# A three-stage attention, mixture and Mish kernel on one core: the element-wise order of its last layer is rearranged

## Chip, cores and metric

One NeuronCore of a Trainium2 chip runs the whole program. The metric is the device time of one execution in microseconds (us); the median of three executions stands for a kernel. The engines are TensorE (PE), VectorE (DVE), ScalarE (ACT), GpSimd (POOL) and SyncE (SP). Each works through its own instructions in program order and waits on semaphores for the others.

## The reference

Three layers follow each other, all in fp32. Attention (2 batches, 8 heads, 768 positions, head size 64) sees 8 global and 96 local keys. A top-2 mixture of 8 experts (512 to 1024 to 512) takes the 1536 tokens, and the last layer is a dense one of 512 to 2048 to 512 with a Mish activation between its two products:

```python
def _moe2_ref(x, w_in, w_out):
    h = x @ w_in
    sp = np.where(h > 20.0, h, np.log1p(np.exp(np.minimum(h, 20.0))))
    g = h * np.tanh(sp)
    return (g @ w_out).astype(np.float32)
```

The change lies in the last layer alone.

## The kernel before

Every fp32 product is made of three products in the fp32r type: each operand is split into a high part (`hi`, a copy rounded to fp32r on ACT) and a low part (`lo`, the rest, by a subtraction on DVE), and PE adds `hi*hi + hi*lo + lo*hi` (`three`, L856 to L860).

The order of the instructions is written by hand: an engine runs its instructions in the order in which the Python code issues them.

**The last layer** works on 4 blocks of 384 tokens (`tb`), with 16 slices of 128 hidden units (`f`) in each: 64 steps, n = 16 tb + f. `last_in` (L1165) makes the 128x384 pre-activations `hp` of a step with 12 matmuls (L858 to L860). `last_out` (L1217) adds the step's slice into three accumulators with 9 matmuls, six from `hhi` (L1225, L1226) and then three from `hlo` (L1230). The loop (L1246) issues on PE `last_in(n)` and then `last_out(n-2)`, so PE has two steps' work between a step's pre-activations and their use. I write in(n) and out(n) for the two.

**The activation** of a step is a chain over ACT and DVE: exp of `hp` on ACT (`mish_0`, L1181); the minimum with e^20 on DVE (L1185), then on ACT the square (L1186), the logarithm (L1187) and `rexp`, an exponential with a negative sign, which gives a first reciprocal (`mish_2`, L1191); three DVE operations, two of them a Newton step (`mish_3`, L1196 to L1198), the third of which multiplies with `hp` and gives the result; its high part on ACT (`mish_5`, L1201) and its low part on DVE (`mish_6`, L1204). In step n the loop issues, leaving conversions aside:

- on ACT: exp(n), high part of n-1, square(n), logarithm(n), rexp(n);
- on DVE: minimum(n), low part of n-1, the three Newton operations of n.

The first and the last step are cut into thirds of 128 columns (`for_cuts`).

**The weight conversions.** The weights of the last layer come as 64-bit words and are turned into `hi` and `lo` by `w64_begin` (L304): for each half tile of 128x512, four DVE operations (L327 to L330) and then `rest` (L321): a copy on ACT (L322) and two DVE operations (L323, L324). 26 of the 32 halves are made in the layers before; six are left and are made in steps 2 to 13: the first two operations in an even step, the next two and `rest` in the odd step behind it. `w64_load` (L296) fetches the next raw half through SP at the end of each odd step.

**The row sums.** For a block after the first, each token's two expert rows are gathered by POOL (`rows_of`, L866, at f = 2, 6, 10 of the block before), weighted and added (`combine_2`, L1155: ACT L1156, DVE L1157, at f = 5, 9, 13), transposed on PE (`combine_3`, L1159: four PE transposes, L1162, at f = 6, 10, 14) and split into `hi` and `lo` (`split_ps`, L862: ACT L863, DVE L864).

Of the kernel before, what the change touches and what calls it, by code (L numbers as in the profile page):

```python
# [9 lines left out]
F32 = mybir.dt.float32  # L10
# [4 lines left out]
AF = mybir.ActivationFunctionType  # L15
OP = mybir.AluOpType
# [5 lines left out]
P = 128  # L22
# [6 lines left out]
TB = 384  # L29
# [147 lines left out]
def build(tc, ctx, I, out, n_global, n_local, dbg=None):  # L177
    nc = tc.nc
    dbg = dbg or {}
    V, A, G, T = nc.vector, nc.scalar, nc.gpsimd, nc.tensor  # L180
# [115 lines left out]
    def w64_load():  # L296
        j, s = divmod(state["load64"], 2)
        if j < 16:
            state["load64"] += 1
            raws[j, s] = wraw.tile([P, 512, 2], I32, name="raw")  # L300
            nc.sync.dma_start(raws[j, s], I["w_moe2"][j, :, s * 512:(s + 1) * 512].bitcast(I32)
                              .rearrange("p (a b) -> p a b", b=2))

    def w64_begin():  # L304


        j, s = divmod(state["conv"], 2)
        if j == 16:
            return None
        state["conv"] += 1  # L310
        if s == 0:
            pool, n = (wlast, "l") if j < 16 - RING else (wring, "")
            pieces[64 + j] = (pool.tile([P, 1024], F32R, name="whi" + n), pool.tile([P, 1024], F32R, name="wlo" + n))
        raw = raws.pop((j, s))
        lw, uw = raw[:, :, 0], raw[:, :, 1]
        hi, lo = (w[:, s * 512:(s + 1) * 512] for w in pieces[64 + j])
        t1 = wtmp.tile([P, 512], I32, name="t1", bufs=2)
        t2 = wtmp.tile([P, 512], I32, name="t2", bufs=1)
        f1 = t1.bitcast(F32)

        def rest():  # L321
            A.activation(hi, f1, AF.Copy)  # L322
            V.tensor_tensor(f1, f1, hi.bitcast(F32), op=OP.subtract)  # L323
            V.tensor_tensor(lo, f1, lo.bitcast(F32), op=OP.add)  # L324

        return (
            lambda: V.tensor_scalar(t1, uw, 0x07FFFFFF, 3, op0=OP.bitwise_and, op1=OP.logical_shift_left),  # L327
            lambda: V.scalar_tensor_tensor(t1, uw, -0x40000000, t1, op0=OP.bitwise_and, op1=OP.bitwise_or),
            lambda: V.tensor_scalar(t2, t1, -0x800000, None, op0=OP.bitwise_and),
            lambda: V.scalar_tensor_tensor(lo, lw.bitcast(U32), 2.0 ** -52, t2.bitcast(F32), op0=OP.mult, op1=OP.mult),  # L330
            rest,
        )

    xgs, xgT = {}, {}
# [46 lines left out]
    with ExitStack() as st:  # L381
# [440 lines left out]
        for t in range(NT):  # L822
            load_raw(t + 2)
            load_values(t + 1)
            for hp in range(0, HP, PER):
# [5 lines left out]
                k = t * HP // PER + hp // PER  # L831
# [34 lines left out]
    def rows_of(t, k):  # L866
        yg = xg_p.tile([P, DM], F32, name="xg") if k == 0 else mk.tile([P, DM], F32, name="ys", bufs=3)
        G.indirect_dma_start(out=yg, out_offset=None, in_=yd[:(E - 1) * CAP, :] if k == 0 else yd,
                             in_offset=bass.IndirectOffsetOnAxis(ap=cidx[:, k, t:t + 1], axis=0))
        return yg  # L870
# [11 lines left out]
    mk = ctx.enter_context(tc.tile_pool(name="mk", bufs=2))  # L882
# [213 lines left out]
    steps = [(e, f) for e in range(E) for f in range(8)]  # L1096
    lists = []
    half = None
    for n, (e, f) in enumerate(steps):
# [39 lines left out]
        half = w64_begin() if conv else None  # L1139
# [13 lines left out]
    gT, acc2 = {}, {}  # L1153

    def combine_2(t, rows):  # L1155
        A.activation(rows[0], rows[0], AF.Copy, scale=wlh[:, 0, t:t + 1])  # L1156
        V.scalar_tensor_tensor(rows[1], rows[1], wlh[:, 1, t:t + 1], rows[0], op0=OP.mult, op1=OP.add)  # L1157

    def combine_3(t, rows, pool, name):  # L1159
        tp = pool.tile([P, 4, P], F32, name=name)  # L1160
        for d in range(4):
            T.transpose(tp[:, d], rows[1][:, d * P:(d + 1) * P], ident)  # L1162
        combine_4(t, tp)

    def last_in(tb, f):  # L1165
        whi, wlo = (w.rearrange("p (d f) -> p d f", d=4) for w in pieces[64 + f // 2 * 2])
        xhi, xlo = x2T[tb]
        c = (f % 2) * P
        hp = ps_h.tile([P, 512], F32, name="hp")
        for d in range(4):  # L1170
            three(hp[:, :TB], whi[:, d, c:c + P], wlo[:, d, c:c + P], xhi[:, d], xlo[:, d], d == 0, d == 3)
        return hp[:, :TB]
# [1 line left out]


    def mish_begin(hp, n):
        r = mk.tile([P, TB], F32, name="r", bufs=1)
        return hp, vt[:, n % 2, :TB], vt[:, 2 + n % 2, :TB], r

    def mish_0(m, cc):  # L1180
        A.activation(m[1][:, cc], m[0][:, cc], AF.Exp)  # L1181
# [11 lines left out]
    def mish_3(m, cc):  # L1193

        h, v, s, r = (a[:, cc] for a in m)
        V.scalar_tensor_tensor(s, s, 1.0, r, op0=OP.add, op1=OP.mult)  # L1196
        V.scalar_tensor_tensor(s, s, -2.0, r, op0=OP.add, op1=OP.mult)
        V.scalar_tensor_tensor(v, s, 0.5, h, op0=OP.add, op1=OP.mult)  # L1198

    def mish_5(m, g, cc):  # L1200
        A.activation(g[0][:, cc], m[1][:, cc], AF.Copy)  # L1201

    def mish_6(m, g, cc):
        V.tensor_tensor(g[1][:, cc], m[1][:, cc], g[0][:, cc].bitcast(F32), op=OP.subtract)  # L1204

    def mish_end():
        return tuple(mk.tile([P, CAP], F32R, name=n)[:, :TB] for n in ("hhi", "hlo"))
# [4 lines left out]
    def for_cuts(n, stage, *a):  # L1212

        for cc in (THIRDS if n in (0, 16 * NTB - 1) else [ALL]):
            stage(*a, cc)

    def last_out(tb, f):  # L1217
        whi, wlo = (w.rearrange("p (f d) -> p f d", f=2)[:, f % 2] for w in pieces[64 + f // 2 * 2 + 1])
        ghi, glo = gT.pop((tb, f))
        last = (tb, f) == steps[-1]  # L1220
        if f == 0:
            acc2[tb] = [ps_a.tile([P, 512], F32, name="ac") for _ in range(TC)]
        for c in range(TC):
            cc = slice(c * P, (c + 1) * P)
            T.matmul(acc2[tb][c], ghi[:, cc], whi, start=(f == 0), stop=False)  # L1225
            T.matmul(acc2[tb][c], ghi[:, cc], wlo, start=False, stop=False)  # L1226
            if last:
                T.matmul(acc2[tb][c], glo[:, cc], whi, start=False, stop=True)
        for c in (() if last else range(TC)):
            T.matmul(acc2[tb][c], glo[:, c * P:(c + 1) * P], whi, start=False, stop=(f == 15))  # L1230

    def last_store(tb, f):
        if f == 15:
            for c in range(TC):
                os = mk.tile([P, DM], F32, name="ys", bufs=3)
                if c % 2:
                    V.tensor_scalar(os, acc2[tb][c], 2.0, None, op0=OP.mult)
                else:
                    A.activation(os, acc2[tb][c], AF.Copy, scale=2.0)
                r0 = tb * TB + c * P  # L1240
                nc.sync.dma_start(out[r0:r0 + P, :], os)

    steps = [(tb, f) for tb in range(NTB) for f in range(16)]
    m = {}
    vt = mk.tile([P, 4, CAP], F32, name="yT", bufs=1)
    for n in range(len(steps) + 2):  # L1246
        new, old = n < len(steps), 1 <= n <= len(steps)
        if new:
            tb, f = steps[n]
            m[n] = mish_begin(last_in(tb, f), n)  # L1250
        if n >= 2:
            last_out(*steps[n - 2])
        if n % 2 == 0:
            half = w64_begin() if n else None
        if new:
            for_cuts(n, mish_0, m[n])
        if old:
            g = gT[steps[n - 1]] = mish_end()
        if old:
            for_cuts(n - 1, mish_5, m[n - 1], g)  # L1260
        if new:
            for_cuts(n, mish_1, m[n])
        if half:
            half[n % 2 * 2]()
        if new:
            for_cuts(n, mish_2, m[n])
        if old:
            for_cuts(n - 1, mish_6, m[n - 1], g)
        if half:
            half[n % 2 * 2 + 1]()  # L1270
        if new:
            for_cuts(n, mish_3, m[n])
        if late and n:
            late.pop(0)()
        if half and n % 2:
            half[4]()
        if n >= 2:
            last_store(*steps[n - 2])
        if new and tb + 1 < NTB:
            for c in range(TC):  # L1280
                t = TC * (tb + 1) + c
                if f == 2 + 4 * c:
                    rows[t] = [rows_of(t, 0), rows_of(t, 1)]
                if f == 5 + 4 * c:
                    combine_2(t, rows[t])
                if f == 6 + 4 * c:
                    combine_3(t, rows[t], ps_q, "tq")
        if n % 2:
            w64_load()

# [2 lines left out]
    with tc.If(most > CAP):  # L1295
        with tc.tile_pool(name="one", bufs=1) as one:
            for tb in range(NTB):
# [4 lines left out]
                for c in range(TC):  # L1302
# [4 lines left out]
                    for d in range(4):  # L1307
# [4 lines left out]
                                    op0=OP.is_equal, op1=OP.mult)  # L1312
                    V.tensor_scalar(g2, iot[:, :E], chosen[:, 1, t:t + 1], w12[:, 1, t:t + 1],
                                    op0=OP.is_equal, op1=OP.mult)
                    V.tensor_tensor(gate[:, c], gate[:, c], g2, op=OP.add)
                V.memset(ysum, 0.0)
                for e in range(E):
                    ac = [ps_a.tile([P, 512], F32, name="ac") for _ in range(TC)]
                    for g in range(4):
# [4 lines left out]
                        for f in range(2):  # L1324
                            hp = ps_h.tile([P, 512], F32, name="hp")
# [11 lines left out]
                vt = mk.tile([P, 4, CAP], F32, name="yT", bufs=1)  # L1337
# [62 lines left out]
```

## Time and profile before

| | us |
|---|---|
| median of 3 runs | 736.98 (736.25 to 737.54) |
| the profiled execution's own time | 739.06 |
| its span, first to last instruction | 737.2 |
| PE busy in the span | 708.8 (96%) |
| DVE busy | 523.9 (71%) |
| ACT busy | 424.0 (58%) |
| the last layer, first matmul (442.3) to the end of the span | 294.9 |

The times in the rows count from the first instruction of the span. A timeline row gives the start, the duration, the engine, the line, the operation, its output and input, the count, and in brackets the idle time of the engine ahead of it and what ended that. The end of a matmul is modelled, so starts are compared rather than ends. For ACT and DVE the start of the next operation can lie before the end of the one ahead.

### The profile page before, as it was taken

The page shows a single profiled execution, that of the slowest core. Times are in us where ns is not written, and L with a number is a line of the kernel's source. Part 1 is how long each engine was busy: PE and PEld are TensorE (multiplying, and loading weights), DVE is VectorE, ACT ScalarE, POOL GpSimd, SP SyncE. Part 2 cuts the span into 40 slices and gives each one's busy share as a digit, 9 for nine tenths or more (in the row PEclk, how much of TensorE's full clock was granted, in tenths as well). Part 3 has the DMA queues.
Part 4 walks back from the last instruction along what each step waited for, and adds up shares of the span by engine and source line. Part 5 has one row for each costly group of instructions (what it writes and reads, how often), then busy time and mean ns, then how long its engine had stood idle before and what let it go on. Part 6 is the DMA issues. An engine that isn't in the chain of part 4 may idle for free.

```text
span 737.2 us, 11732 instructions
## 1 busy us (share of the span) xinstructions
PE 708.8 (96%) x4259; PEld 643.7 (87%) x4259; DVE 523.9 (71%) x1237; ACT 424.0 (58%) x892; POOL 61.6 (8%) x83
## 2 busy tenths in 40 slices
PE   8999899999999999999999989898999999999995
PEld 4777779999999999999999978787999989989993
DVE  7789769977586676758575876888666666666663
ACT  5899632444444544444444437566667667667663
POOL 2000200301010100101000212100120020000000
PEclk9999899999999999999999999999999999999998
DMA  7799321757475655647454734300120030001001
GB/s 166 217 220 240 127 67 39 244 159 232 161 221 167 198 186 177 221 158 219 151 170 142 236 106 135 112 29 0 56 74 1 0 106 10 0 1 44 1 0 47
DMA packets 42932, 89.26 MB, mean 121 GB/s; under 512 B 5987, under 2 KB 18403, under 8 KB 42868
## 3 DMA queue, kind: packets, MB, share of 16 engines
q1 hardware_dynamic: 35412, 69.37, 31.4%
q0 software_dynamic: 4096, 13.11, 5.9%
q10 hardware_dynamic: 3360, 5.97, 2.1%
q8 instruction: 35, 0.57, 0.3%
q14 instruction: 29, 0.24, 0.1%
HBM read 75.32 MB, written 13.11 MB: 120 GB/s over the span
## 4 chain that ended last, share of the span: by engine, by line
PE 79%; DVE 10%; ACT 6%; DMA 2%; issue 1%; POOL 1%; ACTq 0%; DVEq 0%
PE hp L858 11%; PE hp L859 11%; PE hp L860 11%; PE ac L858 6%; PE ac L860 6%; PE ac L859 6%; PE ac L1225 5%; PE ac L1226 5%; PE ac L1230 4%; PE xp L567 3%; PE tp L554 2%; PE sp L516 2%; PE tq L892 2%; PE tq L934 2%; ACT r L1187 1%
## 5 line engine op out<-in xcount | busy, mean ns | idle before, releaser
L858 PE MATMUL hp<-xgh,whi 128*128 128x416 f32 (+1 forms) x288 | 104.2, 362 | 0.0
L280 DVE TENSOR_TENSOR wlo<-raw,whi 128x1024 fp32r<-128x1024 f32 x61 | 74.6, 1223 | 38.1 <-ACT whi L277 35.9
L859 PE MATMUL hp<-xgl,whi 128*128 128x416 f32 (+1 forms) x288 | 100.6, 349 | 0.2 <-DVE xgl L711 0.2
L860 PE MATMUL hp<-xgh,wlo 128*128 128x416 f32 (+1 forms) x288 | 100.7, 350 | 0.0
L858 PE MATMUL ac<-hhi,whi 128*128 128x416 f32 x256 | 92.0, 359 | 0.0
L859 PE MATMUL ac<-hlo,whi 128*128 128x416 f32 x256 | 90.1, 352 | 0.3 <-DVE hlo L905 0.3
L860 PE MATMUL ac<-hhi,wlo 128*128 128x416 f32 x256 | 90.1, 352 | 0.0
L1196 DVE SCALAR_TENSOR_TENSOR yT<-yT,r 128x384 f32<-128x384 f32 (+1 forms) x68 | 36.4, 535 | 73.9 <-ACT r L1191 69.9
L858 PE MATMUL hp<-xgh,whil 128*128 128x384 f32 x224 | 77.0, 344 | 0.0
L859 PE MATMUL hp<-xgl,whil 128*128 128x384 f32 x224 | 76.4, 341 | 0.0
L904 ACT ACTIVATE hhi<-hp 128x416 fp32r<-128x416 f32 x64 | 33.3, 520 | 74.7 <-PE hp L860 64.6
L860 PE MATMUL hp<-xgh,wlol 128*128 128x384 f32 x224 | 75.9, 339 | 0.0
L277 ACT ACTIVATE whi<-raw 128x1024 fp32r<-128x1024 f32 x61 | 64.4, 1055 | 17.2 <-PE ac L859 12.0
L1225 PE MATMUL ac<-whil,hhi 128*128 128x512 f32 x144 | 57.3, 398 | 1.5 <-ACT hhi L1201 1.3
L1226 PE MATMUL ac<-wlol,hhi 128*128 128x512 f32 x144 | 56.6, 393 | 0.0
L859 PEld LDWEIGHTS hp<-xgl,whi 128*128 128x128 f32 x288 | 54.3, 189 | 1.1 <-DVE xgl L711 0.4
L858 PEld LDWEIGHTS hp<-xgh,whi 128*128 128x128 f32 x288 | 54.2, 188 | 1.1 <-ACT xgh L710 0.4
L1181 ACT ACTIVATE yT<-hp 128x384 f32<-128x384 f32 (+1 forms) x68 | 31.6, 471 | 40.6 <-PE hp L860 37.4
L860 PEld LDWEIGHTS hp<-xgh,wlo 128*128 128x128 f32 x288 | 54.0, 188 | 0.4
L863 ACT ACTIVATE xgh<-tq 128x512 fp32r<-128x512 f32 (+2 forms) x38 | 20.2, 533 | 57.8 <-PE tq L892 57.8
L1201 ACT ACTIVATE hhi<-yT 128x384 fp32r<-128x384 f32 (+1 forms) x68 | 34.5, 507 | 31.7 <-DVE yT L1198 30.7
L905 DVE SCALAR_TENSOR_TENSOR hlo<-hp,hhi 128x416 fp32r<-128x416 f32 x64 | 37.5, 586 | 16.7 <-ACT hhi L904 16.7
(241 smaller groups left out, 1526.2 us busy)
## 6 DMA issues: line engine op xcount, KB each, us to landing
raw<-in_w_moe SPq DMA_DIRECT2D x96, 512.0 KB
yd<-ys ACTq DMA_DIRECT2D x21, 256.0 KB
ks<-in_k_t SPq DMA_DIRECT2D x24, 136.0 KB
qr<-in_q_t SPq DMA_DIRECT2D x24, 128.0 KB
vt<-in_v_w SPq DMA_DIRECT2D x12, 256.0 KB
xd<-xs SPq DMA_DIRECT2D x12, 256.0 KB
out<-ys SPq DMA_DIRECT2D x12, 256.0 KB
vt<-in_v_w SPq DMA_DIRECT2D x10, 208.0 KB
```

Of the source, the lines that this page charges most:

```text
L277: A.activation(hi, raw, AF.Copy)
L280: e_lo.tensor_tensor(lo, raw, hi.bitcast(F32), op=OP.subtract)
L858: T.matmul(ps, whi, xhi, start=first, stop=False)
L859: T.matmul(ps, whi, xlo, start=False, stop=False)
L860: T.matmul(ps, wlo, xhi, start=False, stop=last)
L904: A.activation(hhi, hp[:, :CAP], AF.Relu)
L905: V.scalar_tensor_tensor(hlo, hp[:, :CAP], 0.0, hhi.bitcast(F32), op0=OP.max, op1=OP.subtract)
L1181: A.activation(m[1][:, cc], m[0][:, cc], AF.Exp)
L1196: V.scalar_tensor_tensor(s, s, 1.0, r, op0=OP.add, op1=OP.mult)
L1201: A.activation(g[0][:, cc], m[1][:, cc], AF.Copy)
L1225: T.matmul(acc2[tb][c], ghi[:, cc], whi, start=(f == 0), stop=False)
L1226: T.matmul(acc2[tb][c], ghi[:, cc], wlo, start=False, stop=False)
```

## The change

Three things of the last layer's loop are rearranged; no operation is added or taken away.

1. The Newton operations and the high part of step n-1 are issued in step n behind the minimum (DVE) and behind rexp (ACT) of step n (`newton`). On ACT a step is now exp(n), square(n), logarithm(n), rexp(n), high part of n-1; on DVE it is minimum(n), Newton of n-1, a conversion operation, low part of n-1, one or two conversion operations. For step 0 Newton stays ahead of the minimum of step 1. The buffers follow: one buffer for exp's output, two for the result, which now stays in the square's buffer, and two for rexp's.
2. The conversions are one list of operations, taken one or two at a time (`convert`): per step one DVE operation ahead of the low part and one behind it, two behind it in every third step, from step 1 on. The ACT copy of a half (`high`) goes with its third operation. The raw half that follows is fetched when a half is begun.
3. `combine_2` is issued at f = 4, 8, 12 instead of 5, 9, 13.

```diff
+        def high():
             A.activation(hi, f1, AF.Copy)
-            V.tensor_tensor(f1, f1, hi.bitcast(F32), op=OP.subtract)
-            V.tensor_tensor(lo, f1, lo.bitcast(F32), op=OP.add)
+        low = (
+            lambda: V.tensor_tensor(f1, f1, hi.bitcast(F32), op=OP.subtract),
+            lambda: V.tensor_tensor(lo, f1, lo.bitcast(F32), op=OP.add),
+        )
...
     def mish_begin(hp, n):
-        r = mk.tile([P, TB], F32, name="r", bufs=1)
-        return hp, vt[:, n % 2, :TB], vt[:, 2 + n % 2, :TB], r
+        r = vt[:, 3, :TB] if n % 2 else mk.tile([P, TB], F32, name="r", bufs=1)
+        return hp, vt[:, 0, :TB], vt[:, 1 + n % 2, :TB], r
...
+    def convert(k):
+        for _ in range(k):
+            if not todo:
+                half = w64_begin()
+                if not half:
+                    return
+                w64_load()
+                todo.extend((*half[:2], *half[5:6], *half[2:4], *half[6:]))
+            while todo:
+                op = todo.popleft()
+                op()
+                if op.__name__ != "high":
+                    break
...
+        def newton(x):
+            g = gT[steps[x]] = mish_end()
+            for_cuts(x, mish_3, m[x])
+            for_cuts(x, mish_5, m[x], g)
         if new:
             for_cuts(n, mish_0, m[n])
-        if old:
-            g = gT[steps[n - 1]] = mish_end()
-        if old:
-            for_cuts(n - 1, mish_5, m[n - 1], g)
+        if n == 1:
+            newton(0)
         if new:
             for_cuts(n, mish_1, m[n])
-        if half:
-            half[n % 2 * 2]()
-        if new:
             for_cuts(n, mish_2, m[n])
         if old:
-            for_cuts(n - 1, mish_6, m[n - 1], g)
-        if half:
-            half[n % 2 * 2 + 1]()
-        if new:
-            for_cuts(n, mish_3, m[n])
+            if n > 1:
+                newton(n - 1)
+            convert(1)
+            for_cuts(n - 1, mish_6, m[n - 1], gT[steps[n - 1]])
+            convert(1 + (n % 3 == 0))
...
-                if f == 5 + 4 * c:
+                if f == 4 + 4 * c:
                     combine_2(t, rows[t])
```

## Rows read from the trace of the kernel before

**Rows 1.** Waits, 440 to 520 us, PE: total, times, longest, in us.

```profile
PE tq L1162 <- DVE ys L1157: 6.8, 3, 3.2
```

**Rows 2.** Timeline of PE: the first matmul or transpose of some steps.

```profile
455.07 0.50 PE L1225 MATMUL ac<-whil,hhi 128*128 128x512 f32 x1 [0.59 <-ACT hhi L1201]
...
457.26 0.33 PE L858 MATMUL hp<-xgh,whil 128*128 128x384 f32 x1
...
473.91 0.66 PE L1162 MATMUL tq<-ident,ys 128*128 128x128 f32 x4 [3.17 <-DVE ys L1157]
474.32 0.55 PE L858 MATMUL hp<-xgh,whil 128*128 128x384 f32 x1
...
480.15 0.33 PE L858 MATMUL hp<-xgh,whil 128*128 128x384 f32 x1
...
513.92 0.63 PE L1162 MATMUL tq<-ident,ys 128*128 128x128 f32 x4 [2.31 <-DVE ys L1157]
...
518.58 0.34 PE L858 MATMUL hp<-xgh,whil 128*128 128x384 f32 x1
...
718.22 0.33 PE L858 MATMUL hp<-xgh,whi 128*128 128x384 f32 x1
```

**Rows 3.** Windows: length, busy time (count) of five engines, granted clock, DMA share, GB/s.

```profile
474.00:478.00 4.00, 4.00 (x16) 4.00 (x17) 3.44 (x8) 2.24 (x4) 0.00 (x0) 0.57 0.00 0
...
726.90:730.40 3.50, 3.27 (x7) 2.06 (x7) 1.14 (x3) 0.89 (x3) 0.00 (x0) 0.52 0.21 77
```

**Rows 4.** Timeline of DVE, the end of step 5 and the minimum of step 6.

```profile
473.11 0.75 DVE L1157 SCALAR_TENSOR_TENSOR ys<-ys,wlh,xg 128x512 f32<-128x512 f32 x1
473.77 0.35 DVE L1185 TENSOR_SCALAR yT<-yT 128x384 f32<-128x384 f32 x1
```

**Rows 5.** Timeline of DVE and ACT, steps 12 and 13 (minimum to low part).

```profile
503.73 0.35 DVE L1185 TENSOR_SCALAR yT<-yT 128x384 f32<-128x384 f32 x1
...
504.00 0.42 DVE L327 TENSOR_SCALAR t<-raw 128x512 int32<-128x512 int32 x1
...
504.12 0.62 ACT L1186 ACTIVATE yT<-yT,one 128x384 f32<-128x384 f32 x1 [1.07 <-DVE yT L1185]
...
504.77 0.62 ACT L1187 ACTIVATE r<-yT,one 128x384 f32<-128x384 f32 x1
...
505.43 0.53 ACT L1191 ACTIVATE r<-r 128x384 f32<-128x384 f32 x1
...
505.86 0.48 ACT L1181 ACTIVATE yT<-hp 128x384 f32<-128x384 f32 x1
...
505.98 0.56 DVE L1196 SCALAR_TENSOR_TENSOR yT<-yT,r 128x384 f32<-128x384 f32 x1 [0.49 <-ACT r L1191]
...
507.17 0.55 DVE L1198 SCALAR_TENSOR_TENSOR yT<-yT,hp 128x384 f32<-128x384 f32 x1
...
507.64 0.35 DVE L1185 TENSOR_SCALAR yT<-yT 128x384 f32<-128x384 f32 x1
...
507.76 0.53 ACT L1201 ACTIVATE hhi<-yT 128x384 fp32r<-128x384 f32 x1 [1.43 <-DVE yT L1198]
...
508.32 0.56 DVE L1204 TENSOR_TENSOR hlo<-yT,hhi 128x384 fp32r<-128x384 f32 x1
```

**Rows 6.** Groups of DVE by line, 440 to 520 us: count, busy us, mean ns.

```profile
L324 DVE TENSOR_TENSOR wlo<-t,wlo 128x512 fp32r<-128x512 f32 x6 | 4.2, 693 | 0.2
...
L327 DVE TENSOR_SCALAR t<-raw 128x512 int32<-128x512 int32 x6 | 2.5, 421 | 0.0
```

**Rows 7.** Timeline of ACT and POOL, steps 2 and 3.

```profile
453.07 0.47 ACT L1181 ACTIVATE yT<-hp 128x384 f32<-128x384 f32 x1
...
455.58 1.44 POOL L868 DMA_INDIRECT ys<-yd,cidx  x1 [28.41 <-ACT yT L1186]
```

**Rows 8.** Timeline of the last step's chain: ACT, DVE.

```profile
720.51 0.62 ACT L1181 ACTIVATE yT<-hp 128x128 f32<-128x128 f32 x3 [1.41 <-PE hp L860]
...
723.96 0.29 DVE L1196 SCALAR_TENSOR_TENSOR yT<-yT,r 128x128 f32<-128x128 f32 x1 [1.83 <-ACT r L1191]
```

More of the change, by code (lines that the diff above doesn't have):

```diff
@@ L321, in rest @@
         def rest():
+            high()
+            for op in low:
+                op()
+        def high():
             A.activation(hi, f1, AF.Copy)
-            V.tensor_tensor(f1, f1, hi.bitcast(F32), op=OP.subtract)
-            V.tensor_tensor(lo, f1, lo.bitcast(F32), op=OP.add)
+        low = (
+            lambda: V.tensor_tensor(f1, f1, hi.bitcast(F32), op=OP.subtract),
+            lambda: V.tensor_tensor(lo, f1, lo.bitcast(F32), op=OP.add),
+        )
         return (
@@ L331, in w64_begin @@
             rest,
+            high,
+            *low,
         )
@@ L1197, in mish_3 @@
         V.scalar_tensor_tensor(s, s, -2.0, r, op0=OP.add, op1=OP.mult)
-        V.scalar_tensor_tensor(v, s, 0.5, h, op0=OP.add, op1=OP.mult)
+        V.scalar_tensor_tensor(s, s, 0.5, h, op0=OP.add, op1=OP.mult)
     def mish_5(m, g, cc):
-        A.activation(g[0][:, cc], m[1][:, cc], AF.Copy)
+        A.activation(g[0][:, cc], m[2][:, cc], AF.Copy)
     def mish_6(m, g, cc):
-        V.tensor_tensor(g[1][:, cc], m[1][:, cc], g[0][:, cc].bitcast(F32), op=OP.subtract)
+        V.tensor_tensor(g[1][:, cc], m[2][:, cc], g[0][:, cc].bitcast(F32), op=OP.subtract)
     def mish_end():
@@ L1244, in build @@
     m = {}
+    todo = deque()
+    def convert(k):
[8 more added lines that the diff above has]
+                op = todo.popleft()
+                op()
+                if op.__name__ != "high":
+                    break
     vt = mk.tile([P, 4, CAP], F32, name="yT", bufs=1)
@@ L1252, in build @@
             last_out(*steps[n - 2])
-        if n % 2 == 0:
-            half = w64_begin() if n else None
+        def newton(x):
+            g = gT[steps[x]] = mish_end()
+            for_cuts(x, mish_3, m[x])
+            for_cuts(x, mish_5, m[x], g)
         if new:
             for_cuts(n, mish_0, m[n])
-        if old:
-            g = gT[steps[n - 1]] = mish_end()
-        if old:
-            for_cuts(n - 1, mish_5, m[n - 1], g)
+        if n == 1:
+            newton(0)
         if new:
             for_cuts(n, mish_1, m[n])
-        if half:
-            half[n % 2 * 2]()
-        if new:
             for_cuts(n, mish_2, m[n])
         if old:
-            for_cuts(n - 1, mish_6, m[n - 1], g)
-        if half:
-            half[n % 2 * 2 + 1]()
-        if new:
-            for_cuts(n, mish_3, m[n])
+            if n > 1:
[3 more added lines that the diff above has]
+            convert(1 + (n % 3 == 0))
         if late and n:
             late.pop(0)()
-        if half and n % 2:
-            half[4]()
         if n >= 2:
@@ L1287, in build @@
                     combine_3(t, rows[t], ps_q, "tq")
-        if n % 2:
-            w64_load()
     most = nc.values_load(over[:1, :1], min_val=0, max_val=2 * NTOK)
```

## The prediction, made before the changed kernel ran

> **What bounds the kernel now.** Read first the starts of PE's steps in the last layer. From in(16) at 518.58 to in(63) at 718.22 lie 47 steps and six groups of transposes, in 199.64 us; a group takes 473.91 to 474.32, 0.41 us [rows 2]. So a step costs (199.64 - 6 x 0.41) / 47 = 4.20 us: PE's own work, which nothing in this change shortens. Of it last_out has 457.26 - 455.07 = 2.2 with a late start, 2.1 without, and last_in the other 2.1 [rows 2]. The steps ahead of that are slower: in(4) to in(16) takes 61.32 [rows 2], where 12 x 4.20 + 3 x 0.41 = 51.6 would do. These 9.7 us are all that can be won in the steady part.
>
> Then read which wait ends last there. Three times PE stands before the row-sum transposes, 6.8 us in total, 3.2 the longest [rows 1]; the first ends at 473.91 after 3.17, the last at 513.92 after 2.31 [rows 2], which leaves 1.3 for the middle one. The sum that they wait for (L1157) is the last DVE operation of step 5, 13 or 9, behind both conversion operations of `rest`; it starts at 473.11 and PE at 473.91 [rows 2, 4]. After the longest of these gaps the granted clock was 0.57 over 474 to 478, that is mostly the lower of its two levels [rows 3], and the step from 474.32 to 480.15 took 5.83, 1.6 more than 4.20 [rows 2]. 6.8 + 1.6 = 8.4 of the 9.7; the rest is PE waiting for a high part, like the 0.59 before out(1) [rows 2].
>
> **The change part by part.**
>
> *Row sums moved up.* The sum goes from the end of step 5 to the end of step 4 (so too 9 to 8, 13 to 12), and the transposes stay in step 6, behind out(4), which needs the low part of step 4, made by DVE in step 5, after the sum. So the transposes never wait for the sum by themselves: the 6.8 and the 1.6 go, unless the wait moves to the parts of step 4. The sum's ACT half now stands ahead of exp(5). Its rows are gathered by POOL; the first second-row gather is issued at 455.58 and takes POOL 1.44 [rows 7]. The new sum starts near 465.4, 8.4 us after that. When data land no row shows: I take no cost; at most the sum would run at its old place, one step (4.2 us) later.
>
> *The chain in the new order.* Slots, from one start to the next: ACT from the minimum on: 503.73, 504.12, 504.77, 505.43, 505.86, so 0.39 + 0.65 + 0.66 + 0.43 = 2.13 until the next ACT operation, now the high part of n-1 [rows 5]. DVE beside it: the minimum's slot 504.00 - 503.73 = 0.27, Newton's three 507.17 - 505.98 = 1.19 to the third, and 507.76 - 507.17 = 0.59 from there to the high part: 2.05 [rows 5]. So the high part starts 2.13 after the minimum; the low part can start 508.32 - 507.76 = 0.56 later, and PE too [rows 5]. In the steady part exp starts 720.51 - 718.22 = 2.29 after in(n) starts [rows 2, 8], the minimum some 0.5 later (exp takes 0.47 [rows 7]), and the high part is ready at 2.29 + 0.5 + 2.13 + 0.56 = 5.5; out(n-1) begins 4.20 + 2.1 = 6.3 after in(n). The new wait has 0.8 to spare. Queued behind it on ACT is exp(n+1), due at 6.5; on DVE the low part, which PE needs six matmuls later. So steps 16 to 62 keep 4.20.
>
> *DVE's load in steps 1 to 16.* A slot is about 0.08 shorter than the duration: 0.27 for 0.35, and 507.64 - 507.17 = 0.47 for 0.55 [rows 5]. Conversion: two operations like L327 (0.42) and four like L324 (0.69) per half [rows 6], 3.09 in slots, 0.52 each; 7 in three steps make 1.20 a step. Minimum, Newton, low part: 0.27 + 1.19 + 0.47 + 0.47 = 2.40. Row sum and its split, 0.75 [rows 4] and about 0.69, three times in 16 steps: 0.25. Waiting for the high part: it allows the low part at 2.69 after the minimum, while Newton and one conversion end at 2.3 to 2.5, so 0.25. Total 4.10 against PE's 4.20 + 0.08: enough, barely.
>
> By the Trainium skill ("VectorE: DVE Perf Modes", section "The DRAIN you can't avoid") a VectorE operation starts only when the pipe of the one before is empty, save where it is not held. The trace goes by the exception: 0.27 after a minimum of 0.35 the next one starts [rows 5]. What the rule would give is rival B.
>
> *Start-up.* Newton(1) now follows minimum(2), which follows exp(2). exp(2) started at 453.07 [rows 7], its ACT queue up to there is unchanged. Minimum(2) 453.6, high part(1) 453.6 + 2.13 = 455.7, PE 456.3: out(1) is 1.2 later than 455.07 [rows 2], and in(4) at 458.5 instead of 457.26. Then I lay ACT, DVE and PE out by these slots, operation by operation in the order of the diff, up to in(16). For example step 5: DVE ends step 4 with the sum at 466.1, minimum(5) starts there, high part(4) at 468.2, ready at 468.8, out(4) due at 468.9. The high part of step n-1 comes ahead of its product by 0.4, 0.5, 0.1, 1.0, 0.3, 0.7, 0.5, 0.2, 0.0, 0.7, 0.0, 0.8, 0.7 us in steps 3 to 15. Four of these are thin; I charge 0.5 us for them together (bounds 0 and, were every step late by what rival B has, 2.5). The copy of a half waits on ACT for its second DVE operation where both fall into one batch (step 9), and holds exp(10) up by some 1 us; it costs nothing because out(9) is still met by 0.2. in(16): 458.5 + 12 x 4.20 + 3 x 0.41 + 0.5 = 510.6, against 518.58: **-8.0 us**.
>
> *Tail.* Before, the last step's Newton starts at 723.96, behind rexp [rows 8]. Now the high part of step 62 comes behind rexp(63) rather than ahead of the square: the ACT chain is some 0.4 earlier, its three rexp thirds are through near 723.9, then come the high part of 62 (0.56 until its low part) and the low part (0.47), and only then Newton(63): 724.9, **+0.9**. The window of the last seven matmuls had a granted clock of 0.52 [rows 3]; PE is through with out(61) at 718.22 + 4.20 = 722.4 and gets the high part of 62 at 723.9 + 0.56 = 724.5, so it now idles for 2 us in one piece and the lower level may fall elsewhere. At full clock throughout the 3.27 us of PE in that window would be 1.6 shorter (-0.7 in all), and with half of out(62) slowed too, 1.0 longer (+1.9). I take +0.9, since the rows show the lower level at this place.
>
> *Sum:* -8.0 + 0.9 = -7.1. The profiled execution took 739.06 with a span of 737.2, so it would take 732.0; the median of the runs shown, 736.98, becomes 729.9.
>
> **The rivals.**
>
> *B, DVE paces the first 16 steps.* If each operation took its full duration, DVE would need 0.35 + 1.19 + 0.56 + 0.56 + 7/3 x 0.60 + 0.27 = 4.33, and some 0.1 of waiting, 4.43 against 4.28: 16 x 0.15 = 2.4, so 732.3. Against it: the starts in [rows 5]. For it: the thin steps above. The page named above would have this. Chance 0.16.
>
> *C, the clock falls in the start-up.* PE idles some 2.0 us before out(1) instead of 0.59 [rows 2]. A gap of 3.17 was followed by the lower level, at a price of 1.6; one of 2.31 was not known to be (513.92 to 518.58 is 4.66, as 4.20 + 0.41) [rows 2, 3]. 731.5. Chance 0.13.
>
> *D, the wait only changes its name.* Transposes no longer wait, but the high parts come late, or the gathered rows do, and by 0.4 us a step over 16 steps the loop gives 6.4 back: 736.3. It is what the step times of before look like where conversions crowd one step in two. Against it: the loads above. Chance 0.07.
>
> *E, slower.* The high part now stands behind rexp(n), so PE's wait hangs on the chain of the step itself: 5.5 of 6.3 us. Should the chain take 6.3 + 0.19 or more, each of the 48 later steps is late by as much, 48 x 0.19 = 9.1, which eats the 7.1 and puts the time at 739.0; from there it decides. Against it: the 5.5 is made of measured starts. Chance 0.06.
>
> **How the numbers follow.** Forecast 0.58, B 0.16, C 0.13, D 0.07, E 0.06. A measurement of this kernel can tell about 0.2% (1.5 us) from no change. Faster: forecast, B and C, 0.87; same: D, 0.07; slower: E, 0.06. The range takes in the tail's full-clock end and none of the 0.5 (729.9 - 1.6 - 0.5 = 727.8) and at the top B and most of C and B together (733.6): about 0.84 of the chance.
>
> **What would show it.** Right: no wait of PE at L1162; PE's wait before out(1) near 2.0; in(16) near 510.6; the granted clock 1.00 from 456 to 520; steps of 4.20 behind; Newton(63) some 0.9 later after exp(63) than the 3.45 of before; the span near 730. Wrong: PE waiting for `hhi` in most of steps 3 to 16 (B, D) or behind step 16 (E); a clock below 1.00 near 457 (C); ACT waiting at L1156 for rows.

## The result, and the profile after

| | before | after |
|---|---|---|
| median of 6 runs (us) | 737.26 (736.25 to 739.4) | 729.83 (727.23 to 731.42) |
| ratio to before, 95% interval | | 0.9899 [0.9874, 0.9923] |
| the profiled execution's own time | 739.06 | 729.5 |
| its span | 737.2 | 727.6 |

The change makes the kernel 7.4 us (1.0%) faster; 729.9 was predicted. The profile says how far the way there was the predicted one.

First PE's waits in the last layer up to step 16, as in [rows 1]: line and what it waited for, then total, times and longest in us. Of the kernel after, 436 to 516 us:

```profile
PE ac L1235 <- ACT hhi L1211: 2.1, 2, 1.7
```

The transposes (now L1172) have no row any more, so PE never waits for a row sum. The 2.1 are both in the start-up. Next PE's timeline, with the lines that answer to [rows 2]: out(1), in(4), in(16) and in(63); start, duration, engine, line and operation, in brackets the idle time ahead and what ended it.

```profile
452.10 0.51 PE L1235 MATMUL ac<-whil,hhi 128*128 128x512 f32 x1 [1.74 <-ACT hhi L1211]
...
455.32 0.53 PE L868 MATMUL hp<-xgh,whil 128*128 128x384 f32 x1
...
507.49 0.34 PE L868 MATMUL hp<-xgh,whil 128*128 128x384 f32 x1
...
707.13 0.33 PE L868 MATMUL hp<-xgh,whi 128*128 128x384 f32 x1
```

From in(16) to in(63) it is 199.64 us, as before to the hundredth. From in(4) to in(16) it is 52.17 instead of 61.32. The duration of 0.53 at 455.32 shows the lower clock there, and the table of windows confirms it (stretch, length, busy time of PE, PEld, DVE, ACT and POOL with instruction counts, granted clock, DMA share, GB/s). Of the kernel after, around out(1) and, for [rows 3], at 474:

```profile
453.00:456.50 3.50, 3.50 (x11) 2.94 (x10) 3.38 (x8) 2.17 (x4) 2.89 (x3) 0.51 0.72 199
474.00:478.00 4.00, 4.00 (x22) 3.63 (x21) 3.40 (x8) 3.15 (x7) 0.00 (x0) 1.00 0.26 89
```

The lower level has gone from 474 and come up beside out(1). Last, the tail, for [rows 8]: exp(63), the wait ahead of out(62), the first Newton operation of step 63, SP's three issues of the final stores in one row, and the last ACT copy of an accumulator.

```profile
709.43 0.61 ACT L1191 ACTIVATE yT<-hp 128x128 f32<-128x128 f32 x3 [1.01 <-PE hp L870]
...
713.35 0.50 PE L1235 MATMUL ac<-whi,hhi 128*128 128x512 f32 x1 [1.86 <-ACT hhi L1211]
...
713.81 0.28 DVE L1206 SCALAR_TENSOR_TENSOR yT<-yT 128x128 f32<-128x128 f32 x1
...
717.93 2.87 SPq L1251 DMA_DIRECT2D out<-ys  x3
...
718.71 0.60 ACT L1249 ACTIVATE ys<-ac 128x512 f32<-128x512 f32 x1 [0.81 <-PE ac L1238]
```

Newton(63) starts 4.38 after exp(63), before 3.45.

**The two profiles side by side.** The span fell by 9.6. Of that 4.1 lie ahead of the last layer: in(0) starts at 438.16 instead of 442.27, in code that is the same. In the other profiles of this study in(0) lies between 437.93 and 440.74 whatever the order behind it, so I count these 4.1 as one execution against another (the profiled execution of the kernel before took 739.06, near the top of its range). From in(0) to in(16) it is 76.31 before and 69.33 after (-7.0), behind it 0, from exp(63) to the start of the last ACT copy 9.73 and 9.28 (-0.45), and from there to the end of the span 6.96 and 8.89 (+1.9).

### The profile page after: what moved, and what is told of

The parts are those of the page before. It is cut to its first block, busy times and chain, and to the rows that moved or that the text cites. A ratio compares the mean times of both kernels' runs of the same rounds, so it can differ in the third digit from the quotient of the medians.

```text
span 727.6 us, 11661 instructions
## 1 busy us (share of the span) xinstructions
PE 703.3 (97%) x4259; PEld 640.2 (88%) x4259; DVE 524.7 (72%) x1237; ACT 421.3 (58%) x892; POOL 61.2 (8%) x83
## 4 chain that ended last, share of the span: by engine, by line
PE 85%; DVE 7%; ACT 3%; DMA 2%; issue 1%; POOL 1%; ACTq 0%; DVEq 0%
PE hp L868 12%; PE hp L869 12%; PE hp L870 12%; PE ac L1235 6%; PE ac L1236 6%; PE ac L1240 6%; PE ac L868 6%; PE ac L870 6%; PE ac L869 6%; PE xp L577 3%; PE tp L564 3%; PE sp L526 2%; PE tq L902 2%; PE tq L944 2%; DMA raw<-in_w_moe 1%; ACT z L550 1%
## 5 line engine op out<-in xcount | busy, mean ns | idle before, releaser
L1214 DVE TENSOR_TENSOR hlo<-yT,hhi 128x384 fp32r<-128x384 f32 (+1 forms) x68 | 36.1, 534 | 33.7 <-ACT hhi L1211 33.1
L1196 ACT ACTIVATE yT<-yT,one 128x384 f32<-128x384 f32 (+1 forms) x68 | 40.6, 597 | 28.5 <-DVE yT L1195 27.2
L1195 DVE TENSOR_SCALAR yT<-yT 128x384 f32<-128x384 f32 (+1 forms) x68 | 23.4, 347 | 42.8 <-ACT yT L1191 42.0
```

What stands on the lines that cost most here:

```text
L1196: A.activation(s, v, AF.Square, bias=one1)
L1214: V.tensor_tensor(g[1][:, cc], m[2][:, cc], g[0][:, cc].bitcast(F32), op=OP.subtract)
```

## The experiments

What the runs were to tell apart: the prediction put 8.4 of the 9.7 us that could be won down to the transposes waiting for late sums. The rival, L in the expectations, is a loop over two engines. Before, Newton of a step waits on DVE for that step's rexp on ACT, which waits for the minimum on DVE, which is queued behind Newton and the conversions of the step ahead; this loop is longer than PE's 4.20 us in steps 2 to 14, so PE must lose the time somewhere, and the transposes are only where it shows. S in the expectations is the prediction's reading: the sums stand too late. Times of steps below are distances from in(0), which takes the differing starts of the layer out. Conversions and row-sum work fall into steps 4 to 16, and PE's own work from in(4) to in(17) is 13 x 4.20 + 3 x 0.41 = 55.8.

**The change alone, twice more.**

> The changed kernel once more, as the yardstick of this chip. Measured so far: ratio 0.990 to before, 729.8 us median (727.2 to 731.4). Its first profile shows the lower clock level from 453.1 to 456.5 us, behind the 1.74 us for which PE waits before out(1); rival C of the prediction puts this at some 1.5 us and says that it need not fall in every execution. If that is so, a second profile without it has in(5) about 1.5 us nearer to in(0) (20.2 instead of 21.7).

Measured: 730.51, ratio 0.9903 [0.9872, 0.9933]. in(4) comes at 16.15 instead of 17.16, in(16) at 67.81 instead of 69.33, and PE waits 1.74 before out(1) as in the other profile. The window at this place has the full clock:

```profile
453.00:456.50 3.50, 3.50 (x17) 3.09 (x18) 3.43 (x7) 2.83 (x6) 2.67 (x3) 1.00 0.54 152
```

> The changed kernel as the yardstick beside the next two: 729.8 to 730.5, ratio 0.990. In two of its profiles so far in(5) lay 21.87 and 20.33 us behind in(0), with and without the lower clock near out(1); a third has one of these two values.

Measured: 729.47, 0.9886 [0.9865, 0.9906]; in(4) 16.14, in(16) 67.78, the clock 1.00 at out(1). So the same code with the same wait goes either way.

**Sums back in their old place**, in the kernel after:

```diff
-                if f == 4 + 4 * c:
+                if f == 5 + 4 * c:
                     combine_2(t, rows[t])
```

> The changed kernel with the row sums back at f = 5, 9, 13. Theory L (what bounded steps 4 to 16 was the ACT and DVE loop of 4.9 us a step, and PE's wait at the transposes only the place where it came to light): the loop now takes about 4.1 to 4.3, DVE is through with the sum 0.3 to 0.5 us before PE has need of it, so 0 to 0.5 us slower than the changed kernel: 730. Theory S (the sums stood too late, and moving them won the 8 us): PE waits again before three groups of transposes, 6.8 us and a clock fall, and the kernel is back near 736.

Measured: 730.62, 0.9901 [0.9872, 0.9930], beside 0.9903 of the change on the same chip. One of the three groups of transposes waits, for 0.31:

```profile
484.84 0.63 PE L1172 MATMUL tq<-ident,ys 128*128 128x128 f32 x4 [0.31 <-DVE ys L1167]
```

in(17) comes at 72.53 instead of 72.00: in the new order late sums cost 0.3 us of waiting, 0.5 in all, not 6.8.

**Sums early alone**, in the kernel before (5 becomes 4 in the same line).

> The kernel before with one edit: the row sums at f = 4, 8, 12. Theory S (the sums stood too late): PE's 6.8 us at the transposes and the 1.6 us of lower clock go, 728 to 729 on a before of 737. Theory L (the ACT and DVE loop of some 4.9 us a step is the bound of steps 2 to 14): the loop is as long as it was, PE waits for high and low parts instead; Newton of step 14 starts where it did, 71 us behind the first exp; in(16) comes at most 2 to 3 us earlier, 734 to 735.

Measured: 736.11, 0.9992 [0.9971, 1.0013], which can't be told from no change; the profile has in(17) at 79.09 instead of 80.50, 1.4 earlier, which the interval doesn't exclude. PE's waits, 436 to 516 us, and below them the row for high parts in the kernel before, 440 to 520 us:

```profile
PE ac L1225 <- ACT hhi L1201: 2.5, 7, 0.6
PE hp L859 <- DVE xgl L864: 1.4, 1, 1.4
PE hp L858 <- ACT xgh L863: 0.9, 1, 0.9
PE ac L1230 <- DVE hlo L1204: 0.5, 3, 0.2
...
PE ac L1225 <- ACT hhi L1201: 1.3, 3, 0.6
```

The row of [rows 1] is gone. Of the 5.3 us that are listed, 1.0 lie ahead of in(4) as before; the other 4.3 are waits under four other names. The view leaves out gaps under 0.15 us: in all PE loses 64.12 - 55.8 = 8.3 us between in(4) and in(17), at the full clock (1.00 from 455 to 520). Is PE itself part of the loop? ACT's waits from 455 to 513 us say no, since all are for DVE and none for PE:

```profile
ACT hhi L1201 <- DVE yT L1198: 11.2, 12, 1.4
ACT yT L1186 <- DVE yT L1185: 7.3, 10, 1.1
ACT yT L1186 <- DVE wlo L324: 1.1, 1, 1.1
```

The view that would have told this ahead is DVE's own waits. Of the kernel before, 455 to 515 us, and then of the kernel after, 458 to 515 us:

```profile
DVE yT L1196 <- ACT r L1191: 6.2, 12, 0.6
```

```profile
DVE yT L1195 <- ACT yT L1191: 3.0, 4, 1.4
DVE hlo L1214 <- ACT hhi L1211: 1.3, 4, 0.3
DVE ys L1167 <- ACT xg L1166: 0.4, 1, 0.4
```

Before, DVE stands 0.5 us before Newton's first operation in twelve steps in a row, waiting for rexp, and in odd steps with two conversion operations queued behind that wait. From Newton's start in step 2 to that in step 14 the kernel before takes (two rows of DVE's timeline)

```profile
456.77 0.56 DVE L1196 SCALAR_TENSOR_TENSOR yT<-yT,r 128x384 f32<-128x384 f32 x1 [0.56 <-ACT r L1191]
...
515.94 0.56 DVE L1196 SCALAR_TENSOR_TENSOR yT<-yT,r 128x384 f32<-128x384 f32 x1 [1.43 <-ACT r L1191]
```

59.17 us, 4.93 a step against PE's 4.20. In this experiment it takes 454.65 to 512.79, 58.14, and PE from in(4) to in(16) exactly 58.14 too: PE follows the loop. Of the kernel after, the row of the wait for rexp is gone.

**New order, conversions in their old places**, in the kernel after (the calls of `convert` replaced by those of before, the fetch at the end of odd steps):

```diff
+        if n % 2 == 0:
+            half = w64_begin() if n else None
...
-            convert(1)
+            if half:
+                half[n % 2 * 2]()
             for_cuts(n - 1, mish_6, m[n - 1], gT[steps[n - 1]])
-            convert(1 + (n % 3 == 0))
+            if half:
+                half[n % 2 * 2 + 1]()
...
+        if half and n % 2:
+            half[4]()
...
+        if n % 2:
+            w64_load()
```

> The changed kernel with the conversions where they were (two operations in an even step, two and the copy with two more in the odd step), Newton and sums as changed. DVE has per pair of steps 2 x 2.40 + 3.1 + waiting 0.5, 4.2 a step, and 0.25 for the sums, in steps 2 to 13: 4.45 against 4.28 of PE. Theory L: 12 x 0.17 = 2, of which the thin reserve takes some: 0 to 2 us slower than the changed kernel, 730 to 732. If the spreading is what counts: back near 735.

Measured: 733.4, 0.9945 [0.9927, 0.9962]. PE waits for high parts, 436 to 516 us (1.76 of it before out(1)):

```profile
PE ac L1235 <- ACT hhi L1211: 3.7, 6, 1.8
```

**Conversions spread, order of before**, sums early (before, with `convert`):

```diff
-        if half:
-            half[n % 2 * 2]()
         if new:
             for_cuts(n, mish_2, m[n])
         if old:
+            convert(1)
             for_cuts(n - 1, mish_6, m[n - 1], g)
-        if half:
-            half[n % 2 * 2 + 1]()
+            convert(1 + (n % 3 == 0))
         if new:
             for_cuts(n, mish_3, m[n])
...
-        if half and n % 2:
-            half[4]()
```

> The kernel before with the conversions spread as in the changed one (both calls behind rexp) and the sums at f = 4, 8, 12, but Newton in its old place, in its own step. Theory L': the gap of DVE before Newton (0.39 + 0.65 + 0.66 + 0.56 = 2.26 us from the minimum on) takes the conversions whole (0.27 + 0.52 + 0.47 + 0.70 = 2.0), so a step costs 2.26 + 1.19 + 0.47 = 3.9 and 0.25 for the sums, below PE's 4.28: steps 4 to 16 at PE's pace, without the later start (1.2), its clock fall (1.5 where it happens) and the later tail (0.9): 2 to 3 us faster than the changed kernel, 727 to 728. Theory N (the move of Newton is what frees the loop): PE still waits for high parts in steps 4 to 16, 732 to 735.

Measured: 729.31, 0.9893 [0.9865, 0.9921]: as fast as the whole change. From in(4) to in(16) PE keeps its pace (51.62); then two waits come, the first for the low part of the transposed rows, the second for the copy of an accumulator:

```profile
508.02 0.44 PE L869 MATMUL hp<-xgl,whil 128*128 128x384 f32 x1 [0.99 <-DVE xgl L874]
...
519.84 0.50 PE L1235 MATMUL ac<-whil,hhi 128*128 128x512 f32 x1 [0.79 <-ACT ys L1249]
```

The four orders next to each other, sums early in all of them, in(4) to in(17) against PE's own 55.8:

| | conversions in pairs of steps | conversions spread |
|---|---|---|
| Newton in its own step | 64.12 (sums alone) | 57.04 |
| Newton behind the next minimum | 59.10 | 55.85 (the change, second profile) |

Either part brings most of it, 5.0 and 7.1 of 8.3; together they reach PE's own work. These are single profiles, all at the full clock in this stretch. Spreading does two things at once: it thins the conversions out (7 DVE operations in three steps instead of 9) and, in the old order, puts all of them ahead of Newton, into the wait for rexp; the runs don't separate the two. Moving the sums adds about 0.5 (56.39 with the sums back). What spreading alone lacks in this table it has in the start-up and the tail, where its chain is the short one: in(4) at 14.99 rather than 16.15, exp(63) to the last copy 8.34 rather than 9.27.

**Newton early at the ends only**: the kernel after, with Newton of the step before ahead of the minimum in steps 1, 2 and 63.

```diff
+    EARLY = (1, 2, len(steps) - 1)
...
-        if n == 1:
-            newton(0)
+        if n in EARLY:
+            newton(n - 1)
...
-            if n > 1:
+            if n not in EARLY:
                 newton(n - 1)
```

> The changed kernel with Newton ahead of the minimum in steps 1, 2 and 63 (new order in steps 3 to 62). If start-up and tail cost what the prediction says: out(1) waits 0.6 instead of 1.7 us, in(4) 0.7 to 1.2 earlier, no lower clock level near out(1); last Newton 3.45 instead of 4.4 us behind the last exp: 1.6 to 3.1 us faster than the changed kernel, 727 to 728. If they are hidden anyway: no change, 729.8.

Measured: 730.27, 0.9887 [0.9857, 0.9917], no gain that can be seen. in(4) is early (14.98), but a wait of 0.79 follows, in(5) comes at 20.21 against 20.33, and in(16) at 67.99 against 67.81: the 1.2 us of the start-up are only put off to the step where Newton changes place. Of the tail's 0.93 only 0.16 came: Newton(63) starts 4.22 after exp(63) instead of 4.38. This isn't the old order there, in which Newton(62) is through in step 62; here its three operations run from 710.18 on, ahead of the minimum of 63 on DVE, which starts 1.16 after exp(63) (710.67) instead of 0.31:

```profile
711.36 0.55 DVE L1208 SCALAR_TENSOR_TENSOR yT<-yT,hp 128x384 f32<-128x384 f32 x1
711.83 0.49 DVE L1195 TENSOR_SCALAR yT<-yT 128x128 f32<-128x128 f32 x3
```

And the last matmuls got the lower clock:

```profile
717.90:721.40 3.50, 3.26 (x7) 2.08 (x7) 1.05 (x3) 0.83 (x3) 0.00 (x0) 0.51 0.21 76
```

**How much the new wait has to spare.** The kernel after, with one or three copies more on ACT ahead of the high part, in steps 17 to 62; they write over a buffer that is no longer needed.

```diff
             for_cuts(n, mish_2, m[n])
+            for _ in range(3 if 16 < n < len(steps) - 1 else 0):
+                A.activation(m[n][1], m[n][0], AF.Copy)
```

> The changed kernel with one more ACT copy of 128x384 behind rexp in steps 17 to 62 (a slot of 0.43 us that nobody needs). The prediction's reserve of the new wait in the steady part is 0.8 us: no change, 729.8, steps of 4.20.

Measured: 730.37, 0.9912 [0.9878, 0.9946]; exp(16) to exp(63) 199.76 against 199.62. One copy (a slot of 0.47) is free. What there is to spare can be read in the kernel after itself:

```profile
601.78 0.51 ACT L1211 ACTIVATE hhi<-yT 128x384 fp32r<-128x384 f32 x1
...
602.32 0.56 DVE L1214 TENSOR_TENSOR hlo<-yT,hhi 128x384 fp32r<-128x384 f32 x1 [0.66 <-ACT hhi L1211]
...
603.15 0.39 PE L1235 MATMUL ac<-whil,hhi 128*128 128x512 f32 x1
```

The high part is there at 602.32, when DVE starts on it, and PE comes to it at 603.15: 0.83 to spare (0.8 predicted). With the one copy more 0.3 are left of it.

> The same with three copies, 1.29 us. They use up the reserve of 0.8, by 0.49. Rival E as written (each of the steps late by the excess): 46 x 0.49 = 22 us slower, 752. Second reading: exp(n), high part n-1, out(n-1), in(n+2) is a ring over two steps, so a step grows by half of it, 46 x 0.25 = 11 us, 741.

Measured: 757.29, 1.027 [1.0232, 1.0307]; exp(16) to exp(63) 225.71, 26.1 longer, on average 0.57 for each of the 46 steps. The timeline of ACT, of PE's first matmul of an out and of the minimum on DVE:

```profile
602.61 1.52 ACT L1293 ACTIVATE yT<-hp 128x384 f32<-128x384 f32 x3
604.02 0.52 ACT L1211 ACTIVATE hhi<-yT 128x384 fp32r<-128x384 f32 x1
604.43 0.48 ACT L1191 ACTIVATE yT<-hp 128x384 f32<-128x384 f32 x1
...
604.59 0.50 PE L1235 MATMUL ac<-whil,hhi 128*128 128x512 f32 x1 [0.94 <-ACT hhi L1211]
...
605.04 0.35 DVE L1195 TENSOR_SCALAR yT<-yT 128x384 f32<-128x384 f32 x1
```

The three copies hold the high part up by 604.02 - 602.61 = 1.41, 0.6 more than there is to spare, and PE now waits for it. But the 0.57 is a mean and not this excess in each step. At the end of the stretch, where ACT has neither row sums nor stores, exp follows exp like this:

```profile
719.49 0.49 ACT L1191 ACTIVATE yT<-hp 128x384 f32<-128x384 f32 x1
...
724.14 0.49 ACT L1191 ACTIVATE yT<-hp 128x384 f32<-128x384 f32 x1
...
728.69 0.49 ACT L1191 ACTIVATE yT<-hp 128x384 f32<-128x384 f32 x1
```

4.65 and 4.55 in turn, 0.40 above 4.20, which lies between the half of the excess (the second reading) and the whole (rival E). Where ACT also has row sums or stores, a step takes up to 5.43. ACT's waits from 522 to 735 us no longer name PE, which in the kernel after was 38.8 us of them from 510 to 707, so ACT's own queue is part of the limit; how much of it, the run doesn't settle. My 22 us were low, and neither of the two readings holds for each step.

**Towards a faster kernel.** First, spreading alone with the transposes one step earlier (`combine_3` at f = 5, 9, 13), against its wait of 0.99.

> Spreading alone (Newton in its old place), with the transposes of the row sums at f = 5, 9, 13 instead of 6, 10, 14. Spreading alone had in(16) at 66.61 us behind in(0), 1.2 before the changed kernel without the clock fall, but then lost 1.23 in step 16, where PE waited 0.99 for the split of the third row sum, the last DVE operation of step 14, and 0.79 at the accumulators' store in step 18. A step earlier the split is out of the way and the two waits go: in(17) near 70.8, in(63) to in(16) 199.6, 1 to 2 us faster than the changed kernel without the clock fall, 728 to 729. If PE now waits for the sum in steps 5, 9 and 13 (0.3 to 1 us each), nothing is won: 730.

Measured: 728.97, 0.9885 [0.9865, 0.9904]. The wait of 0.99 is gone, of the 0.79 0.3 are left, and the wait for a sum is back in step 5:

```profile
464.50 0.66 PE L1172 MATMUL tq<-ident,ys 128*128 128x128 f32 x4 [1.51 <-DVE ys L1167]
```

Then the last store, issued by ACT behind its own copy instead of by SP:

```diff
-                nc.sync.dma_start(out[r0:r0 + P, :], os)
+                (nc.scalar if (tb, c) == (NTB - 1, 2) else nc.sync).dma_start(out[r0:r0 + P, :], os)
```

> The one before, with the last of the three stores at the end issued by ACT, behind its own copy, instead of SP. In the changed kernel the issue of that store on SP took 1.47 us where the two ahead of it took 0.33, and the span ended 8.9 us behind the start of the last ACT copy instead of 7.0. If the issue waits for SP's own earlier stores, ACT's queue is free of that: 1.0 to 1.4 us faster than the one before, 727. If it waits for the transfers themselves, no change.

Measured: 727.92, 0.9875 [0.9856, 0.9895]. By the trace, from the start of the last copy to the end of the span 6.4 us instead of 8.15; the two medians lie 1.05 apart with overlapping intervals. The last copy and its issue:

```profile
718.90 0.60 ACT L1249 ACTIVATE ys<-ac 128x512 f32<-128x512 f32 x1 [0.79 <-PE ac L1238]
719.52 0.37 ACTq L1251 DMA_DIRECT2D out<-ys  x1
```

Last, the first transposes back to f = 6, the others at 9 and 13.

> The version that the runs point to: spreading alone, Newton in its old place, the last store issued by ACT, and the transposes of the row sums at f = 6, 9, 13. In the run before, PE waited 1.51 us for the first sum in step 5 and for no other; at f = 6 that wait goes, so in(16) near 66.9 instead of 68.45 behind in(0), and the time some 1.5 us below its 727.9: 726 to 727, 2 to 3 us below the changed kernel. If DVE has not the room, the wait only moves on to step 9: 728.

Measured: 726.8 (725.58 to 728.25), 0.9845 [0.9822, 0.9868], the fastest of all. But the last edit is not what did it: the wait went from step 5 to step 9,

```profile
482.50 0.63 PE L1172 MATMUL tq<-ident,ys 128*128 128x128 f32 x4 [1.57 <-DVE ys L1167]
```

and in(17) comes at 72.50 against 72.64. Up to in(63) this kernel is even 1.3 behind the change at the full clock (268.78 against 267.45 from in(0)). Against the change (0.9886 to 0.9903 in three timings) its ratio is 0.4% to 0.6% lower, and only one of the three intervals overlaps with it; the shorter end of the store is the part of that which a trace shows.

## Why the prediction was right, point by point

**The bound** was read rightly: 199.64 behind step 16 before and after, and the 9.7 us ahead of it were what could be won.

**The attribution failed.** The step is "So the transposes never wait for the sum by themselves: the 6.8 and the 1.6 go, unless the wait moves to the parts of step 4". Moving the sums alone wins nothing that can be measured (0.9992; 1.4 us in the profile), and leaving them late in the new order costs 0.5 us in the trace. The 6.8 in [rows 1] were the place at which the lateness of a loop over ACT and DVE (4.93 us a step) surfaced on PE; what shortened the loop were Newton's move and the spread conversions, in the runs 5.0 and 7.1 us, each without the other. The number came out right all the same because the steps were laid out with the whole new order, and that layout had PE as its bound.

**The loop term** of 9.7 was delivered in full, less the clock: from in(5) to in(16) after takes 47.46, and 11 x 4.20 + 3 x 0.41 = 47.43. The layout by slots is what carried the number. The thirteen leads of the high part over its product in steps 3 to 15 measure, in the second profile of the change (from the start of the high part plus 0.56 to the product's first matmul), 0.58, 0.67, 0.31, 1.20, 0.62, 0.76, 0.58, 0.29, 0.18, 0.75, 0.12, 1.00 and 0.81 us: the forecast pattern, each 0.05 to 0.32 more. So no step ran out, and the **0.5 for thin steps** was not needed, it measures 0.0.

**Rival B** did not come. DVE is busy 48.05 of the 51.66 us from in(4) to in(16) in the second profile, 4.00 a step, and waits 0.1 a step for the high part: the 4.10 held, with the overlap of neighbouring operations (the 3.09 for a half is 3.12 by its own terms, which changes nothing). By the Trainium skill ("VectorE: DVE Perf Modes", section "The DRAIN you can't avoid") an operation that is held starts only when the pipe is empty. The starts here stay earlier than that, which the section allows for one that is not held, and as in [rows 5]: in the run with three copies the minimum of 605.04 lasts 0.35 and Newton starts at 605.31. **Rival D**, the wait under other names, is what the sums alone got.

**The start-up** of +1.2: out(1) was to come 14.0 after in(0) and came 13.94 after it; in(4) +1.16 at the full clock. On top of it came **rival C** in the first profile: in(5) at 21.87 against 20.33, 1.54 where 1.6 was priced. It had a chance of 0.13 as one outcome for the kernel. It is an outcome of an execution: it shows in 4 of 7 profiles with the new start-up (the wait is 1.74 to 1.76 in all seven), and in none of 7 with the old one, where the wait is 0.55 to 0.6.

**The tail**: Newton(63) +0.93, with +0.9 predicted, and a wait of 1.86 for the high part of 62, with 2 predicted. That the lower level might move elsewhere was a bound; in the profile of after the clock is full to the last matmul, so the last copy comes 0.45 earlier after exp(63) rather than 0.9 later (0.7 earlier was the bound for this). A term that the sum doesn't have took that back: +1.9 from the last copy to the end of the span. The 0.9 itself shows where the clock is full on both sides: exp(63) to the last copy is 9.27 in the second profile of the change and 8.34 in spreading alone.

**The reserve** of 0.8 behind step 16 is 0.8 in the kernel after. **Rival E** did not come, and its law (the whole excess, each step) isn't borne out: with an excess of 0.6 the steps without other work on ACT grew by 0.40.

**The sum.** From in(0) to in(16) -8.0 was predicted; the three profiles of the change have -7.0, -8.5 and -8.5. The tail's +0.9 was -0.45 + 1.9 = +1.5, then +1.7 and +0.3, since the end behind the last copy took 8.89, 9.14 and 7.74 against 6.96. In all -5.5, -6.8 and -8.2, against -7.1 predicted and -7.4 in the medians. So the size is right, but single executions of one kernel lie that far apart, by where the clock falls and by the last store, and the agreement to 0.1 us is partly luck: a term that wasn't needed (0.5), a fall of the clock in some executions (1.5) and an end that nobody priced (0.8 to 2.2) offset each other.

## What to carry to other kernels

A wait that ends last tells where lateness surfaces, not where it is made: if two engines go round in a loop of their own, follow both engines' waits and compare start to start of one operation over many steps with the bound engine's step, before the wait is blamed. Here DVE's wait for rexp, twelve times 0.5 us, named the loop; taking away PE's visible wait mostly gave it other names. Of several parts of a change, ask for each what it is worth alone; two that shorten the same loop don't add up.

## What was not expected of the hardware

**The third of three close stores.** SP's three final issues end 1.49 us after the last copy in the profile of after (717.93 + 2.87 = 720.80 against 718.71 + 0.60 = 719.31), and 0.35 after it before (the two rows of the kernel before):

```profile
728.30 2.89 SPq L1241 DMA_DIRECT2D out<-ys  x3
...
730.24 0.60 ACT L1239 ACTIVATE ys<-ac 128x512 f32<-128x512 f32 x1 [1.96 <-PE ac L1228]
```

The third issue itself takes 1.47, and in eight other profiles with the issues 0.8 and 0.6 us apart 1.19 to 1.75, against 0.33 in the kernel before with wider gaps. In these nine the span ends 7.7 to 9.2 us after the start of the last copy, in the three with 0.33 7.0 to 7.3. Close gaps alone are not the cause: with the sums alone moved the gaps are as close, and the three issues take 1.71 in all, the third 0.33. Issued by ACT it took 0.37. Why is left open.

**The clock beside out(1).** After the same wait of 1.74 us it fell to the lower level (0.51) in one execution of this kernel and stayed at 1.00 in another. The Trainium skill ("TensorE: Matmul & The Clock Gate", section "What's actually happening") says of a kernel's first matmuls that the number of slow ones varies from run to run; the profiles here show such a variation in the middle of a kernel, at 1.5 us a time.
